# Early attention blocks: queries with places of their own, keys in pairs of blocks, and new durations in the plan of the first stage

## The chip, the core and the metric

The kernel runs on one core of a Trainium2 chip. The metric is the device time of one execution in microseconds (us); lower is better. A core has TensorE (matmuls, called PE in the profile, and its weight loads, PEld), VectorE (DVE), ScalarE (ACT), GpSimd (POOL) and SyncE (SP, which here issues most DMAs). Each engine takes its instructions in the order in which the program lists them and waits on semaphores for the others. TensorE accumulates in PSUM; everything else that is local lies in SBUF.

## The reference, cut to what matters

Three layers follow each other: attention with a window of 128 positions, a dense feed-forward layer, and a layer of 8 experts of which each token uses one.

```python
# q, k, v: (4, 8, 576, 64) float32
scores = scale * np.matmul(q, k.transpose(0, 1, 3, 2))
mask = (rel >= 0) & (rel < window)
scores = np.where(mask, scores + bias[None], -1000000000.0)
...
attn = attn / (np.sum(attn, axis=-1, keepdims=True) + 1e-09)
attn_out = np.matmul(attn, v)
# x: (2304, 512), w_in: (512, 2048), w_out: (2048, 512)
h = x @ w_in
g = h - np.tanh(h)
x = g @ w_out
# then: every token goes to the one of 8 experts with the largest logit
```

The 2304 tokens are 18 blocks of 128. A block's queries see the keys of their own block and of the block before (block 0, and others that start a sequence, see their own alone).

## The kernel before, in words

**The work.** The tokens go in groups of two blocks (a group is g, its blocks b = 2g and 2g + 1). For a block, `quarter` handles two heads at a time, so a block has four quarters (a = 4b + 0 to 3; the half hf names four heads, qq the pair in it, jj = 0, 1 the head of the pair). The heads of a pair lie in partitions 0 to 63 and 64 to 127 of the transposed queries and keys. A quarter makes scores on TensorE, adds the bias and takes the minimum of the negated scores on VectorE (`soft`, L479), takes the exponential on ScalarE (`exp`, L493), transposes the probabilities and multiplies them by the values. Then `x_out` (L628 to L641) transposes the block's output for the feed-forward layer, whose `step` handles one of eight pairs of feature blocks (fp): h = x w_in (L681), the nonlinearity on ScalarE and VectorE (L686 to L698), and the product with w_out into `acc` (L705).

**Early blocks.** Blocks 0 to 3 (NF = 4) are early: their attention is done in f32 (`early`), with transposes on TensorE (`tr_pe`, L513), copies out of PSUM (`tr_out`, L519) and f32 values (`pv_f`, L530). Their scores (L452) are one matmul of 128 columns for each head and key block; in the trace an f32 matmul leaves two records, a transpose one. Later blocks use another number format and a DMA transpose (`tr`, L508).

**Borrowed places.** Early data lies in the SBUF places of weights that are loaded later. A place is called by its tag: `wi12` holds w_in's feature block 12, `wo15` w_out's 15 (FT = 16 of each). Before the change, `wo15` and `wo14` hold the keys of blocks 0, 1 and 2, 3 (`kf[0]`, `kf[1]`, loaded by L391), `wi14` and `wi13` the values, and `wi15` a second buffer for probabilities. Queries (L395) have two places, `qst0` and `qst1`, each for half a block, used in turn, so a load must wait for the scores two halves before. The `slots` in `weight` name what must have been read before a weight may be loaded into its place.

**Weights.** The 32 weight blocks of the feed-forward layer come as 64-bit integers and are rebuilt by `weight`: a load (L298, L300), a conversion on ScalarE (L325), a scaling (L307 on ScalarE or L309 on VectorE), two joining instructions on VectorE (L328, L331), a rounded copy (L313) and a subtraction for the remainder (L317, on VectorE or GpSimd). Both halves must be there before `step` may use the block.

**The plan.** Nothing is issued while the tasks are described. `Plan.add` takes for each task the engines that may do it with a duration for each, a due time, and what it reads and writes. `Plan.order` then builds the whole program's order: again and again it takes, of all tasks whose inputs are ready, the one with the earliest start, then the earliest due time, then the first described, on the engine that would finish it first. A load on SP also waits until the modelled transfer pipe is nearly free. So the durations that tasks are given decide the order of the instructions on every engine, and where there is a choice the engine. `weights` and `qk_half` and `quarter` set due times from the step number p at which a block is wanted.

In `build`, group 0 gets four of the eight pairs first, then group 1 all eight, then group 0 the other four, then the other groups. The lines that decide a plan's choice are these:

```python
fin = {e: max(free.get(e, 0.0), r0) + c + ALPHA * load.get(e, 0.0) for e, c in eng.items()}
e = min(fin, key=fin.get)
st = max(free.get(e, 0.0), r0)
if e == "SP":
    st = max(st, pipe - AHEAD)
key = (st, due, n)
```

Of the kernel before, what the change touches and what calls it, by code (L numbers as in the profile page):

```python
# [10 lines left out]
F32 = mybir.dt.float32  # L11
# [22 lines left out]
FT = FF // 128  # L34
# [4 lines left out]
NF = 4  # L39
# [9 lines left out]
QK = 2  # L49
# [113 lines left out]
class Builder:  # L163
# [122 lines left out]
    def weight(self, P, j, kind, f, due):  # L286
# [31 lines left out]

        slots = [("kf", 2 * (FT - 1 - f) + x, y) for x in range(2) for y in range(2)] if kind == "o" else []
        if (kind, f) == ("i", FT - 1):  # L320
            slots = [("p32", 1, 0), ("p32", 1, 1)]
        elif kind == "i":
            slots = [("vf", 2 * (FT - 2 - f) + x) for x in range(2)]
        P.add({"SP": 1.46}, load, due - 2 - (EARLY if self.early() else 0), w=[raw, (raw, "L")] + slots)
        P.add({"ACT": 0.46}, lambda e: nc.scalar.activation(  # L325
            out=v["L"], in_=v["L"].bitcast(U32), func=AF.Copy, scale=7.499 * 2.0 ** -32), due, r=[raw], w=[(raw, "L")])
        P.add({"DVE": 0.335, "ACT": 0.46}, scale, due, r=[raw, "at"], w=[wf])
        P.add({"DVE": 0.6}, lambda e: nc.vector.scalar_tensor_tensor(  # L328
            out=v["L"], in0=v["H"], scalar=-2 ** 31, in1=v["L"], op0=ALU.bitwise_and, op1=ALU.bitwise_or),
            due, r=[raw], w=[(raw, "L")])  # L330
        P.add({"DVE": 0.6}, lambda e: nc.vector.scalar_tensor_tensor(  # L331
            out=fi, in0=fi, scalar=3, in1=v["L"], op0=ALU.logical_shift_left, op1=ALU.bitwise_or), due,
            r=[raw, (raw, "L"), "at"], w=[wf])
        P.add({"ACT": 0.46, "DVE": 0.335}, hi, due, r=[wf, "at"], w=[raw, (raw, "L"), (key, 0)])
        P.add({"DVE": 0.6, "POOL": 1.23}, lo, due, r=[wf, (key, 0), "at"], w=[(key, 1)])

# [8 lines left out]
    def qk_half(self, P, b, hf, due):  # L345
# [33 lines left out]
        if b >= NF:  # L379
            q, qn = ("q", b, hf), ("q", n)  # L380
            P.add({"SP": 0.73}, lambda e: load("q"), due - 2, r=["at"], w=[q, "stq"])
            P.add({"ACT": 0.52}, qcopy, due, r=["at", q, "stq"], w=[qn])
            P.add(sub, qsub, due, r=["at", qn, "stq"], w=[("ql", n)])
        else:
            s4 = b % 4

            def load_k0(e):
                if hf == 0 and s4 % 2 == 0 and b < 4:
                    self.kf[s4 // 2] = self.wp.tile([128, 2, 4, 128], F32, tag=f"wo{FT - 1 - s4 // 2}",
                                                    name=f"kf{s4 // 2}")  # L390
                nc.sync.dma_start(out=self.kf[s4 // 2][:, s4 % 2, hf * 2:hf * 2 + 2, :], in_=self.i["k0"][b, hf])  # L391

            def load_q0(e):
                self.qst[n] = self.at.tile([128, 2, 4, 128], F32, tag=f"qst{n}", name=f"qf{n}", bufs=1)
                nc.sync.dma_start(out=self.qst[n][:, 0, 0:2, :], in_=self.i["q0"][b, hf])  # L395

            P.add({"SP": 0.36}, load_k0, due - 2, r=["at"], w=[("kf", s4, hf)] + ([("kf", s4 + x, y) for x in range(2) for y in range(2)] if hf == 0 and s4 % 2 == 0 and b < 4 else []))
            P.add({"SP": 0.36}, load_q0, due - 2, r=["at"], w=[("q", n), ("ql", n)])

# [31 lines left out]
    def quarter(self, P, a, due):  # L431
# [13 lines left out]
        def scores(jj):  # L445
            sc = v["sc"][jj] = self.scores[jj][:, 0]
            q = self.qst[n]
            j = qq + 2 * jj
            hp, p0 = hf * 4 + j, 64 * jj
            if b < NF:  # L450
                for x in [b] if one else [b - 1, b]:
                    nc.tensor.matmul(sc[:, b - x, :], lhsT=q[p0:p0 + 64, 0, qq, :],  # L452
                                     rhs=self.kf[x % 4 // 2][p0:p0 + 64, x % 2, hf * 2 + qq, :], start=True, stop=True)
                return
            sl = s if one else slice(0, 2)
# [117 lines left out]
        q = [("q", n), ("ql", n)]  # L573
        ttr = 0.2 if one else (0.35 if s == 0 else 0.48)
        ttr += 0.13 * (2 * (b in SPLIT) + (b - 1 in SPLIT))
        for jj in range(2):
            if early:
                P.add({"PE": 0.4 if one else 0.8}, lambda e, jj=jj: scores(jj), due,
                      r=["at"] + [("kf", x % 4, hf) for x in ([b] if one else [b - 1, b])] + q, w=[("sc", jj)])
# [6 lines left out]
        for jj in range(2):  # L586
            P.add({"ACT": 0.33 if one else 0.45}, lambda e, jj=jj: exp(jj), due,
                  r=["at", ("sc", jj), ("mx", jj, a % 2)], w=[("p32", pb, jj), ("sm", sk, qq, jj)])
        sm = [("sm", sk, x, y) for x in range(2) for y in range(2)]
        half = [("xr", 2 * hf), ("xr", 2 * hf + 1)]  # L590
        if early:
            for jj in range(2):
                P.add({"PE": 0.15 if one else 0.25}, lambda e, jj=jj: tr_pe(jj), due, r=["at", "con", ("p32", pb, jj)],
                      w=[("tp", jj)])
            for jj in range(2):
                P.add({"ACT": 0.3, "DVE": 0.22} if one else {"ACT": 0.4, "DVE": 0.35}, lambda e, jj=jj: tr_out(e, jj),
                      due, r=["at", ("tp", jj)], w=[("pt", a % 2, 1)] if jj else [("pt", a % 2), ("pt", a % 2, 1)])
            P.add({"PE": 0.6 if one else 1.2}, pv_f, due,
                  r=["at", ("pt", a % 2), ("pt", a % 2, 1)] + [("vf", x) for x in ([b] if one else [b - 1, b])], w=[("o", qq)] if qq else ["o", ("o", 0), ("o", 1)])
            if qq:  # L600
                P.add({"DVE": 0.5}, recip, due, r=["at"], w=sm)
                P.add({"DVE": 0.4}, mul, due, r=["at", "o", ("o", 0), ("o", 1)] + sm, w=half if hf else [("xr", m) for m in range(4)])
            return
# [557 lines left out]
    def build(self):  # L1161
        tc, nc = self.tc, self.nc
        for n in ("kf", "vf", "sums", "oh4", "qst", "xr", "acc", "w"):
            setattr(self, n, {})
# [24 lines left out]
        for g, fps in visits:  # L1189
# [173 lines left out]
def layout(inputs):  # L1363
    f = np.float32

    def compact(x):
        y = np.asarray(x).reshape(B, 2, 4, S, D)[:, :, HPOS]
        y = y.transpose(1, 2, 4, 0, 3).reshape(2, 2, 2, D, NB, 128)[:, :, :, :, :NF]
        return np.ascontiguousarray(y.transpose(4, 0, 1, 3, 2, 5).reshape(NF, 2, 128, 256))

# [41 lines left out]
```

## Time and profile before

| what | value |
|---|---|
| median of 3 runs | 858.4 us (857.5 to 860.28) |
| the profiled execution | 856.46 us |
| its span, first to last instruction | 854.8 us |
| mean granted TensorE clock | 0.987 of 2.4 GHz |
| TensorE busy | 820.6 us (96%) |
| VectorE busy | 575.4 us (67%) |
| ScalarE busy | 437.9 us (51%) |
| GpSimd busy | 232.0 us (27%) |

The span lies 1.66 us below the execution's own time, which is counted from outside. Busy shares are averages over the whole span; the early attention, the rebuilding of the weights and the first feed-forward steps fill about the first 140 us, and what bounds the kernel there is read from that stretch alone. In the profile a matmul's end is modelled, so that the durations of neighbouring records overlap; the distance between their starts tells more. The granted clock is given in parts of 2.4 GHz: 1.00 is 2.4 GHz and 0.50 is 1.2 GHz. In the chain of waits each piece is what released the next; "issue" is time in which an engine waited for nothing that the profile shows.

### The profile page before, as it was taken

The page shows a single profiled execution, that of the slowest core. Times are in us where ns is not written, and L with a number is a line of the kernel's source. Part 1 is how long each engine was busy: PE and PEld are TensorE (multiplying, and loading weights), DVE is VectorE, ACT ScalarE, POOL GpSimd, SP SyncE. Part 2 cuts the span into 40 slices and gives each one's busy share as a digit, 9 for nine tenths or more (in the row PEclk, how much of TensorE's full clock was granted, in tenths as well). Part 3 has the DMA queues.
Part 4 walks back from the last instruction along what each step waited for, and adds up shares of the span by engine and source line. Part 5 has one row for each costly group of instructions (what it writes and reads, how often), then busy time and mean ns, then how long its engine had stood idle before and what let it go on. Part 6 is the DMA issues. An engine that isn't in the chain of part 4 may idle for free.

```text
span 854.8 us, 15357 instructions
## 1 busy us (share of the span) xinstructions
PE 820.6 (96%) x5292; PEld 731.2 (86%) x5292; DVE 575.4 (67%) x1525; ACT 437.9 (51%) x990; POOL 232.0 (27%) x228
## 2 busy tenths in 40 slices
PE   7998799999999999999999999999999999999995
PEld 5886688989889998898888898998889999989994
DVE  5688997777769567777677675577366655666230
ACT  4587765554555455555555543455255544545120
POOL 1255742133325123243333251022110110111011
PEclk9998799999999999999999999999999999999998
DMA  7786316934433234333334322265266655655000
GB/s 246 248 281 234 96 55 156 301 99 118 99 94 96 79 69 117 75 87 88 97 83 91 91 51 50 99 213 167 77 205 221 200 184 178 197 166 173 19 27 30
DMA packets 110327, 112.35 MB, mean 131 GB/s; under 512 B 62997, under 2 KB 77333, under 8 KB 110112
## 3 DMA queue, kind: packets, MB, share of 16 engines
q1 hardware_dynamic: 107104, 101.82, 41.8%
q0 software_dynamic: 3136, 9.46, 3.0%
q8 instruction: 43, 0.70, 0.3%
q14 instruction: 44, 0.36, 0.1%
HBM read 86.59 MB, written 17.48 MB: 122 GB/s over the span
## 4 chain that ended last, share of the span: by engine, by line
PE 73%; DVE 10%; issue 7%; DMA 6%; SPq 2%; ACT 2%; POOL 1%; POOLq 0%; ACTq 0%; DVEq 0%
PE h L681 19%; PE acc L705 17%; PE he L1009 10%; PE y L1044 8%; PE o L541 3%; DMA pt<-ph 3%; PE sc L452 3%; DVE wst L331 2%; DMA out<-yo,ix 2%; PE sc L457 2%; PE y L1040 2%; PE of L530 2%; PE misc L780 1%; SPq L914 1%; PE sc L513 1%
## 5 line engine op out<-in xcount | busy, mean ns | idle before, releaser
L681 PE MATMUL h<-xT,wi 128*128 128x256 f32 x1728 | 228.9, 287 | 0.0
L681 PEld LDWEIGHTS h<-xT,wi 128*128 128x128 f32 x1728 | 220.3, 194 | 5.2 <-issue 0.2
L705 PE MATMUL acc<-wo,gh 128*128 128x512 f32 x576 | 187.0, 406 | 0.6 <-ACT xspill L657 0.6
L705 PE MATMUL acc<-wo,gl 128*128 128x512 f32 x288 | 113.8, 395 | 0.1
L705 PEld LDWEIGHTS acc<-wo,gh 128*128 128x128 f32 x576 | 100.4, 191 | 15.1 <-ACT xspill L657 0.8
L686 ACT ACTIVATE t<-h 128x512 f32<-128x512 f32 x72 | 43.0, 597 | 113.6 <-PE h L681 113.5
L1044 PE MATMUL y<-eo,ge 128*128 128x512 f32 x336 | 88.5, 399 | 0.0
L479 DVE CUSTOM_DVE_ANT_0 sc<-sc,bias 128x256 f32<-128x256 f32 (+1 forms) x144 | 52.4, 375 | 44.4 <-PE sc L457 34.7
L493 ACT ACTIVATE p<-sc,mx 128x256 f32<-128x256 f32 (+1 forms) x128 | 59.1, 464 | 33.7 <-DVE mx L479 31.3
L1069 POOL DMA_INDIRECT out<-yo,ix x24 | 23.1, 964 | 177.2 <-PE y L1040 61.7
L698 DVE TENSOR_TENSOR gl<-t,gh 128x512 fp32r<-128x512 f32 x72 | 65.1, 904 | 7.4 <-ACT gh L694 7.3
L1044 PEld LDWEIGHTS y<-eo,ge 128*128 128x128 f32 x336 | 60.0, 188 | 9.7
L1031 DVE SCALAR_TENSOR_TENSOR ge<-he,ge 128x256 fp32r<-128x256 f32 x104 | 30.0, 326 | 54.7 <-ACT ge L1025 54.6
L705 PEld LDWEIGHTS acc<-wo,gl 128*128 128x128 f32 x288 | 54.6, 190 | 13.1 <-DVE gl L698 0.5
L943 DVE TENSOR_TENSOR eo<-est,eo 128x512 fp32r<-128x512 f32 x58 | 43.7, 755 | 27.0 <-ACT eo L939 25.1
L1025 ACT ACTIVATE ge<-he 128x320 fp32r<-128x320 f32 (+1 forms) x56 | 24.1, 430 | 71.5 <-PE he L1009 66.3
L1009 PE MATMUL he<-xT,ei 128*128 128x320 f32 x384 | 60.4, 309 | 0.0
L1009 PEld LDWEIGHTS he<-xT,ei 128*128 128x128 f32 x384 | 58.3, 188 | 2.3
L689 DVE TENSOR_TENSOR t<-h,t 128x512 f32<-128x512 f32 x72 | 49.4, 686 | 14.8 <-ACT t L686 14.5
L1009 PE MATMUL he<-xA,ei 128*128 128x320 f32 (+1 forms) x384 | 59.0, 302 | 0.0
L939 ACT CAST eo<-est 128x512 fp32r<-128x512 f32 x64 | 39.7, 621 | 36.8 <-PE y L1040 22.5
L1009 PEld LDWEIGHTS he<-xA,ei 128*128 128x128 f32 x384 | 56.3, 188 | 2.6
(182 smaller groups left out, 1409.6 us busy)
## 6 DMA issues: line engine op xcount, KB each, us to landing
est<-in_w SPq DMA_DIRECT2D x128, 256.0 KB
rawi<-in_w_in SPq DMA_DIRECT2D x16, 512.0 KB
rawo<-in_w_out SPq DMA_DIRECT2D x16, 512.0 KB
stk<-in_k SPq DMA_DIRECT2D x30, 256.0 KB
stq<-in_q SPq DMA_DIRECT2D x28, 256.0 KB
bucket<-in_c_pad SPq DMA_DIRECT2D x8, 771.0 KB
xe<-bucket SPq DMA_DIRECT2D x17, 257.0 KB
vst<-in_v SPq DMA_DIRECT2D x30, 128.0 KB
```

What stands on the lines that cost most here:

```text
L479: nc.vector.tensor_tensor_reduce(out=x, in0=x, in1=self.bias[:, h, c0:c1], scale=-0.125, scalar=mx[:, 1:2] if m else 3.0e38, op0=ALU.add, ...
L493: nc.scalar.activation(out=v["p32"][:, jj * W:(jj + 1) * W], in_=x, func=AF.Exp, scale=-1.0, bias=v["mx"][jj][:, 0:1], accum_out=self.sums ...
L681: nc.tensor.matmul(h3(v["h"], f2), lhsT=w[:, a, k, :], rhs=xT[c][:, :, k, :], start=(k == 0 and n == 0), stop=(k == KD - 1 and n == 2))
L686: nc.scalar.activation(out=v["t"], in_=v["h"].rearrange("p a b -> p (a b)"), func=AF.Tanh)
L689: nc.vector.tensor_tensor(out=v["t"], in0=v["h"].rearrange("p a b -> p (a b)"), in1=v["t"], op=ALU.subtract)
L698: self.eng(e).tensor_tensor(out=v["gl"], in0=v["t"], in1=v["gh"].bitcast(F32), op=ALU.subtract)
L705: nc.tensor.matmul(self.acc[g, t], lhsT=v[a][:, c0:c0 + 128], rhs=self.w["o", fs[f2]][:, c, :], start=(first and f2 == 0 and n == 0), stop ...
L939: nc.scalar.copy(out=t[:, 0, :], in_=v["x"])
L943: self.eng(eng).tensor_tensor(out=t[:, 1, :], in0=v["x"], in1=t[:, 0, :].bitcast(F32), op=ALU.subtract)
L1009: nc.tensor.matmul(h[:, 0:N], lhsT=w[:, a, c0:c0 + 128], rhs=xT()[b][:, k, 0:N], start=(k == 0 and n == 0), stop=(k == KD - 1 and n == 2))
L1031: nc.vector.scalar_tensor_tensor(out=g[:, o:o + c1 - c0], in0=hk[f][:, c0:c1], scalar=0.0, in1=g[:, c0:c1].bitcast(F32), op0=ALU.max, op1= ...
L1044: nc.tensor.matmul(y[t], lhsT=gt(f, a)[:, (t - ts[0]) * 128:(t - ts[0] + 1) * 128], rhs=self.w["o", f0 + f][:, b, :], start=(f == 0 and n ...
```

## The change

It has three parts. Queries of the early blocks get places for whole blocks: `wi12` for blocks 0 and 1, `wo12` for 2 and 3, one load for a block. Keys get a place for each pair of a block with the one before: `wo15` for blocks 0 and 1, `wo14` for 1 and 2, `wo13` for 2 and 3; blocks 2 and 3 load the block before once more. A head's scores then are one matmul of 256 columns (128 for block 0). Loads of the weights that follow into these places wait for their new readers (`slots`). The third part are the durations: those of the weights' tasks, of the softmax (for all blocks, the later ones too), and of the early blocks' matmuls and copies. The input arrays q0 and k0 are laid out for it on the host.

```diff
+        slots = {("i", FT - 1): [("p32", 1, 0), ("p32", 1, 1)], ("i", FT - 2): [("vf", 0), ("vf", 1)],
+                 ("i", FT - 3): [("vf", 2), ("vf", 3)], ("i", FT - 4): [("qf", 0), ("qf", 1)],
+                 ("o", FT - 4): [("qf", 2), ("qf", 3)]}.get(key, [])
+        if kind == "o" and 1 <= FT - f < NF:
+            slots = [("kf", FT - f, 0), ("kf", FT - f, 1)]
...
-        P.add({"ACT": 0.46}, lambda e: nc.scalar.activation(
+        P.add({"ACT": 0.68}, lambda e: nc.scalar.activation(
...
-        P.add({"DVE": 0.335, "ACT": 0.46}, scale, due, r=[raw, "at"], w=[wf])
-        P.add({"DVE": 0.6}, lambda e: nc.vector.scalar_tensor_tensor(
+        P.add({"DVE": 0.5, "ACT": 0.68}, scale, due, r=[raw, "at"], w=[wf])
+        P.add({"DVE": 1.0}, lambda e: nc.vector.scalar_tensor_tensor(
...
-        P.add({"DVE": 0.6}, lambda e: nc.vector.scalar_tensor_tensor(
+        P.add({"DVE": 0.92}, lambda e: nc.vector.scalar_tensor_tensor(
...
-        P.add({"ACT": 0.46, "DVE": 0.335}, hi, due, r=[wf, "at"], w=[raw, (raw, "L"), (key, 0)])
-        P.add({"DVE": 0.6, "POOL": 1.23}, lo, due, r=[wf, (key, 0), "at"], w=[(key, 1)])
+        P.add({"ACT": 0.62, "DVE": 0.47}, hi, due, r=[wf, "at"], w=[raw, (raw, "L"), (key, 0)])
+        P.add({"DVE": 0.95, "POOL": 1.45}, lo, due, r=[wf, (key, 0), "at"], w=[(key, 1)])
...
+    def qk_early(self, P, b, due):
+
+        nc, d2 = self.nc, b // 2
+
+        def load_k(e):
+            t = max(b, 1)
+            if b != 1:
+                self.kf[t] = self.wp.tile([128, 2, 4, 128], F32, tag=f"wo{FT - t}", name=f"kf{t}")
+            for x in ([b] if b < 2 else [b, b - 1]):
+                nc.sync.dma_start(out=self.kf[t][:, t - x], in_=self.i["k0"][x])
+
+        def load_q(e):
+            if b % 2 == 0:
+                self.qf[d2] = self.wp.tile([128, 2, 4, 128], F32, tag=f"w{'io'[d2]}{FT - 4}", name=f"qf{d2}")
+            nc.sync.dma_start(out=self.qf[d2][:, b % 2], in_=self.i["q0"][b])
+
+        P.add({"SP": 0.73}, load_q, due, r=["at"], w=[("qf", b)] + ([] if b % 2 else [("qf", b + 1)]))
+        P.add({"SP": 0.73 if b < 2 else 1.46}, load_k, due, r=["at"],
+              w=[("kf", 1, 0)] if b == 1 else [("kf", max(b, 1), 0), ("kf", max(b, 1), 1)])
...
-            if b < NF:
-                for x in [b] if one else [b - 1, b]:
-                    nc.tensor.matmul(sc[:, b - x, :], lhsT=q[p0:p0 + 64, 0, qq, :],
-                                     rhs=self.kf[x % 4 // 2][p0:p0 + 64, x % 2, hf * 2 + qq, :], start=True, stop=True)
+            if early:
+                x = slice(1, 2) if one else slice(0, 2)
+                nc.tensor.matmul(sc[:, 0:W // 128, :], lhsT=self.qf[b // 2][p0:p0 + 64, b % 2, hf * 2 + qq, :],
+                                 rhs=self.kf[max(b, 1)][p0:p0 + 64, x, hf * 2 + qq, :], start=True, stop=True)
                 return
...
-        ttr = 0.2 if one else (0.35 if s == 0 else 0.48)
+        ttr = 0.43 if one else (0.57 if cs == 0 else 0.8)
...
-                P.add({"PE": 0.4 if one else 0.8}, lambda e, jj=jj: scores(jj), due,
+                P.add({"PE": 0.45 if one else 0.65}, lambda e, jj=jj: scores(jj), due,
...
-            P.add({"ACT": 0.33 if one else 0.45}, lambda e, jj=jj: exp(jj), due,
+            P.add({"ACT": 0.57 if one else 0.67}, lambda e, jj=jj: exp(jj), due,
...
-                P.add({"PE": 0.15 if one else 0.25}, lambda e, jj=jj: tr_pe(jj), due, r=["at", "con", ("p32", pb, jj)],
+                P.add({"PE": 0.28 if one else 0.5}, lambda e, jj=jj: tr_pe(jj), due, r=["at", "con", ("p32", pb, jj)],
...
-                P.add({"ACT": 0.3, "DVE": 0.22} if one else {"ACT": 0.4, "DVE": 0.35}, lambda e, jj=jj: tr_out(e, jj),
+                P.add({"ACT": 0.3, "DVE": 0.29} if one else {"ACT": 0.38, "DVE": 0.42}, lambda e, jj=jj: tr_out(e, jj),
...
-            P.add({"PE": 0.6 if one else 1.2}, pv_f, due,
+            P.add({"PE": 0.85 if one else 1.65}, pv_f, due,
...
+                            self.qk_early(P, b, due - QK - 2)
```

## Rows read from the trace of the kernel before

**Rows 1.** The page's head and first part: busy us, share, instructions.

```profile
span 854.8 us, 15357 instructions
PE 820.6 (96%) x5292; PEld 731.2 (86%) x5292; DVE 575.4 (67%) x1525; ACT 437.9 (51%) x990; POOL 232.0 (27%) x228
```

**Rows 2.** Stretches: length, busy us (x) by engine, granted clock, DMA share, GB/s.

```profile
core 0: us, PE busy (x) PEld busy (x) DVE busy (x) ACT busy (x) POOL busy (x), PEclk, DMA share, GB/s
0.00:16.00 16.00, 9.66 (x35) 6.97 (x35) 8.57 (x39) 5.82 (x18) 2.07 (x26) 1.00 0.78 237
16.00:56.00 40.00, 40.00 (x163) 32.41 (x161) 29.23 (x73) 27.38 (x73) 15.04 (x13) 1.00 0.78 258
56.00:108.00 52.00, 41.83 (x246) 36.17 (x245) 49.72 (x81) 40.62 (x90) 31.76 (x22) 0.84 0.55 188
...
140.00:840.00 700.00, 694.53 (x4638) 625.59 (x4637) 460.04 (x1281) 343.75 (x769) 167.72 (x156) 1.00 0.43 122
```

**Rows 3.** The chain that ended last, early pieces: start us, us, what.

```profile
6.83 0.72 PE sc L452 x2
...
30.31 1.90 PE of L530 x8
32.21 0.43 PE sc L513 x2
32.63 1.15 PE sc L452 x4
33.78 0.62 PE sc L513 x2
...
125.43 0.69 DVE wo L317
```

**Rows 4.** TensorE's instructions in order of time: start us, us, what.

```profile
4.66 0.80 PE L452 MATMUL sc<-kf,qf 64*128 64x128 f32 x4 [4.66 <-DMA qf<-in_q]
...
6.76 0.79 PE L452 MATMUL sc<-kf,qf 64*128 64x128 f32 x2
...
17.71 0.53 PE L530 MATMUL of<-vf,ptf 128*128 128x64 f32 x2
...
52.08 2.79 PE L681 MATMUL h<-xT,wi 128*128 128x256 f32 x12
...
56.73 1.69 PE L681 MATMUL h<-xT,wi 128*128 128x256 f32 x12
...
71.49 2.91 PE L681 MATMUL h<-xT,wi 128*128 128x256 f32 x12
...
81.33 0.72 PE L452 MATMUL sc<-kf,qf 64*128 64x128 f32 x8
```

**Rows 5.** A stretch behind the first fall of the granted clock, columns as in rows 2.

```profile
68.00:74.00 6.00, 5.70 (x26) 5.48 (x26) 5.12 (x13) 4.33 (x11) 2.79 (x2) 0.52 1.05 391
```

**Rows 6.** Line 530's records, 16 to 52 us: duration ns, least, median, most.

```profile
L530 PE MATMUL of<-vf,ptf x48: 316/421/473, 17.7 to 48.4; 128*128 128x64 f32 x48
```

**Rows 7.** SyncE's queue, 0 to 140 us: us waited in total, times, longest.

```profile
SPq L395 <- PE sc L452: 20.4, 6, 7.5
```

**Rows 8.** TensorE's waits, 0 to 140 us: us in total, times, longest.

```profile
PE sc L513 <- ACT p32x L493: 4.9, 3, 3.7
PE sc L452 <- DMA qf<-in_q: 4.7, 1, 4.7
PE misc L628 <- DVE xr L567: 4.3, 2, 3.7
```

**Rows 9.** VectorE's instructions near 86 us: start us, us, what.

```profile
85.67 0.68 DVE L328 SCALAR_TENSOR_TENSOR rawo<-rawo 128x512 int32<-128x512 int32 x1
86.27 0.42 DVE L479 CUSTOM_DVE_ANT_0 sc<-sc,bias 128x256 f32<-128x256 f32 x1
...
89.64 1.79 DVE L328 SCALAR_TENSOR_TENSOR rawo<-rawo 128x512 int32<-128x512 int32 x1
```

**Rows 10.** TensorE's waits, 140 to 854 us, as in rows 8.

```profile
PE o L541 <- DMA pt<-ph: 4.1, 6, 1.0
```

More of the change, by code (lines that the diff above doesn't have):

```diff
@@ L317, in lo @@
             self.eng(e).tensor_tensor(out=t[:, 1, :], in0=f32, in1=t[:, 0, :].bitcast(F32), op=ALU.subtract)
[L319 to L323, printed above, removed]
+        slots = {("i", FT - 1): [("p32", 1, 0), ("p32", 1, 1)], ("i", FT - 2): [("vf", 0), ("vf", 1)],
[3 more added lines that the diff above has]
+            slots = [("kf", FT - f, 0), ("kf", FT - f, 1)]
         P.add({"SP": 1.46}, load, due - 2 - (EARLY if self.early() else 0), w=[raw, (raw, "L")] + slots)
-        P.add({"ACT": 0.46}, lambda e: nc.scalar.activation(
+        P.add({"ACT": 0.68}, lambda e: nc.scalar.activation(
             out=v["L"], in_=v["L"].bitcast(U32), func=AF.Copy, scale=7.499 * 2.0 ** -32), due, r=[raw], w=[(raw, "L")])
-        P.add({"DVE": 0.335, "ACT": 0.46}, scale, due, r=[raw, "at"], w=[wf])
-        P.add({"DVE": 0.6}, lambda e: nc.vector.scalar_tensor_tensor(
+        P.add({"DVE": 0.5, "ACT": 0.68}, scale, due, r=[raw, "at"], w=[wf])
+        P.add({"DVE": 1.0}, lambda e: nc.vector.scalar_tensor_tensor(
             out=v["L"], in0=v["H"], scalar=-2 ** 31, in1=v["L"], op0=ALU.bitwise_and, op1=ALU.bitwise_or),
             due, r=[raw], w=[(raw, "L")])
-        P.add({"DVE": 0.6}, lambda e: nc.vector.scalar_tensor_tensor(
+        P.add({"DVE": 0.92}, lambda e: nc.vector.scalar_tensor_tensor(
             out=fi, in0=fi, scalar=3, in1=v["L"], op0=ALU.logical_shift_left, op1=ALU.bitwise_or), due,
             r=[raw, (raw, "L"), "at"], w=[wf])
-        P.add({"ACT": 0.46, "DVE": 0.335}, hi, due, r=[wf, "at"], w=[raw, (raw, "L"), (key, 0)])
-        P.add({"DVE": 0.6, "POOL": 1.23}, lo, due, r=[wf, (key, 0), "at"], w=[(key, 1)])
+        P.add({"ACT": 0.62, "DVE": 0.47}, hi, due, r=[wf, "at"], w=[raw, (raw, "L"), (key, 0)])
+        P.add({"DVE": 0.95, "POOL": 1.45}, lo, due, r=[wf, (key, 0), "at"], w=[(key, 1)])
     def early(self):
@@ L383, in qk_half @@
             P.add(sub, qsub, due, r=["at", qn, "stq"], w=[("ql", n)])
[L384 to L398, printed above, removed]
+    def qk_early(self, P, b, due):
[13 more added lines that the diff above has]
+              w=[("kf", 1, 0)] if b == 1 else [("kf", max(b, 1), 0), ("kf", max(b, 1), 1)])
     def v_full(self, P, b, due):
@@ L446, in scores @@
             sc = v["sc"][jj] = self.scores[jj][:, 0]
-            q = self.qst[n]
             j = qq + 2 * jj
             hp, p0 = hf * 4 + j, 64 * jj
-            if b < NF:
-                for x in [b] if one else [b - 1, b]:
-                    nc.tensor.matmul(sc[:, b - x, :], lhsT=q[p0:p0 + 64, 0, qq, :],
-                                     rhs=self.kf[x % 4 // 2][p0:p0 + 64, x % 2, hf * 2 + qq, :], start=True, stop=True)
+            if early:
+                x = slice(1, 2) if one else slice(0, 2)
+                nc.tensor.matmul(sc[:, 0:W // 128, :], lhsT=self.qf[b // 2][p0:p0 + 64, b % 2, hf * 2 + qq, :],
+                                 rhs=self.kf[max(b, 1)][p0:p0 + 64, x, hf * 2 + qq, :], start=True, stop=True)
                 return
+            q = self.qst[n]
             sl = s if one else slice(0, 2)
@@ L577, in quarter @@
             if early:
-                P.add({"PE": 0.4 if one else 0.8}, lambda e, jj=jj: scores(jj), due,
-                      r=["at"] + [("kf", x % 4, hf) for x in ([b] if one else [b - 1, b])] + q, w=[("sc", jj)])
+                P.add({"PE": 0.45 if one else 0.65}, lambda e, jj=jj: scores(jj), due,
+                      r=["at", ("qf", b)] + [("kf", max(b, 1), x) for x in ([1] if one else [0, 1])], w=[("sc", jj)])
             else:
@@ L1162, in build @@
         tc, nc = self.tc, self.nc
-        for n in ("kf", "vf", "sums", "oh4", "qst", "xr", "acc", "w"):
+        for n in ("kf", "qf", "vf", "sums", "oh4", "qst", "xr", "acc", "w"):
             setattr(self, n, {})
@@ L1368, in compact @@
         y = y.transpose(1, 2, 4, 0, 3).reshape(2, 2, 2, D, NB, 128)[:, :, :, :, :NF]
-        return np.ascontiguousarray(y.transpose(4, 0, 1, 3, 2, 5).reshape(NF, 2, 128, 256))
+        return np.ascontiguousarray(y.transpose(4, 1, 3, 0, 2, 5).reshape(NF, 128, 4, 128))
     def tr(x):
```

## The prediction

> **What bounds the kernel now.** I went from the page to stretches, then to the chain of waits, then to single instructions. The page: TensorE is busy 820.6 of 854.8 us [rows 1], so the end can move only where TensorE idles, runs slowly or gets less to do. The table of stretches shows where that is [rows 2]. From 140 to 840 us TensorE is busy 694.5 of 700 us. From 16 to 56 us it is busy all 40.00 us, with VectorE at 29.23. From 56 to 108 us VectorE is busy 49.72 of 52 and TensorE 41.83. So there are two early bounds: TensorE during the softmax attention of blocks 0 to 2, then VectorE, which joins the weights' two integer halves. Whatever ends earlier there, the full queue of matmuls behind it ends earlier by.
>
> From 30.31 us the chain is TensorE alone [rows 3]: a quarter of two heads costs 1.90 (probabilities times values) + 0.43 + 1.15 + 0.62 + 1.15 (transposes and scores in turn, the second head's scores as the first's) = 5.25 us.
>
> The clock has to be read with care. The granted clock stands at 1.00 (2.4 GHz) in the rows up to 56 us [rows 2], yet twelve records of h take 2.79 us at 52.08 and 1.69 at 56.73 [rows 4]; at 71.49 they take 2.91 in a stretch whose granted clock is 0.52, mostly the 1.2 GHz level [rows 4, 5]. By the durations all of 16 to 54 us ran at the lower level; it rose after the first run of full-width h matmuls. It fell again behind idle time: 0.52 from 68 to 74 us [rows 5], and the whole of 56 to 108 us has 0.84 [rows 2].
>
> **The change, part by part.** *Keys in pairs.* For a block that sees two key blocks, each head's scores are now one matmul of 256 columns instead of two of 128. A matmul in f32 leaves two records, so four records of 128 become two of 256. What is a record of 256 worth? At the low level a head with four records holds the chain for 1.15 us and one with two for 0.72 [rows 3], so one more record of 128 columns costs 0.215. Two readings are open. If weights are the limit, 256 columns also cost 0.215, as the 256-column records of h do: (2.79 - 0.42) / 11 = 0.215, with 0.42 for the last one [rows 4, 6]. If columns are the limit, they cost 0.43 and nothing is saved. The row that decides is the pair of 64-column records at 17.71, 0.53 us in all [rows 4]: the second begins 0.53 - 0.42 = 0.11 after the first, because its weights had been loaded early. So 64 columns of f32 take 0.11, two clocks a column at 1.2 GHz, and 128 take 0.215 with nothing left over. I take 0.43 for 256: the merge itself is worth **0**. The other end is 0.43 less a head.
>
> By the Trainium skill ("TensorE: Matmul & The Clock Gate", Back-to-back issue gap) consecutive matmuls are N/1.2 ns apart on the cold clock, one clock a column; that gives 0.21 us for 256 columns and would make the merge worth 0.43 a head. The pair at 17.71 speaks against it for f32; no run so far shows 256 columns of f32.
>
> *The two heads of a quarter side by side.* They lie in partitions 0 to 63 and 64 to 127. Where both heads' scores follow each other they overlap: four records of two heads take 0.80 us at 4.66 and two records of one head 0.79 at 6.76 [rows 4]: the second head is free. So in a quarter whose heads are split by a transpose, 1.15 us is lost at the low level. From 16 to 52 us all fourteen heads stand alone as at 32.63, a transpose before and behind [rows 3]: seven quarters, up to 7 x 1.15 = 8.05 us. Does the new plan put them together? The plan places by earliest start, then due time. It had charged 1.2 for the probabilities times values; now 1.65, and an exponential 0.67 instead of 0.45. While the 1.65 run, both heads' exponentials can end; then the two transposes and the two scores are all ready when TensorE comes free, and equal due times leave the scores adjacent. With the old charges the second head was not ready in time, so a transpose came between. Weight instructions on VectorE can still part them; I take four quarters of seven, **-4.6**; ends 0 and -8.05. VectorE has 10.8 us free in that stretch and the DMA share is 0.78 [rows 2], so both can follow into 35 us; without that room the term is nothing.
>
> *Queries in places of their own.* Eight loads of 128 KB become four of 256 KB, and none waits for an earlier reader. SyncE's queue stood 20.4 us in six such waits, the longest 7.5 [rows 7], with weight loads queued behind. TensorE did not wait on these except for the first load, and VectorE, not the data, is late after 56 us. I take 0; an earlier weight could save up to the two stalls below.
>
> *What it adds on queues.* Two further key loads of 256 KB (blocks 2 and 3 fetch the block before again): 0.5 MB at 258 GB/s [rows 2] is 2 us of transfer, taken as 0 beside the freed SyncE time; otherwise 2 us that delay weights. The first scores now need 512 KB instead of 256 KB. TensorE waited 4.7 us for the smaller loads [rows 8]; 0.25 MB more at the 237 and 258 GB/s of the first stretches [rows 2] costs 1.0 to 1.1, less if the transfers are not yet at their pace: **+0.9**, in full, nothing covers it. All eight query and key transfers have early due times, so the first weight starts behind them by about 1.5 MB more, 5 us; VectorE is idle then (8.57 of 16 us busy [rows 2]).
>
> *Weights in the borrowed places.* Two more weights of the last two of eight pairs wait for block 3's scores (the last begin at 81.33 us [rows 4]). They are needed by the second token group's last steps, after 140 us; hidden, unless SyncE holds other loads behind them.
>
> *The plan's times.* The joining instructions were planned at 0.6 and are now 0.92 to 1.0; they took 0.68 alone and 1.79 beside a GpSimd subtraction [rows 9]. Because the plan ran ahead of VectorE, weight work stood ahead of a softmax at 86.27, and TensorE waited 3.7 us for its probabilities; 3.7 more for the block's output near 100 us [rows 8]. True charges should let the softmax, with its earlier due time, go first. That is 7.4 us if both go. But VectorE's work stays the same, so part returns as later weights: I take a third, **-2.5**; ends +4 (one more stall of that size) and -7.4. The longer softmax charges also hold for the later blocks, where TensorE waits 4.1 us in six waits on transposed probabilities [rows 10]; a reordering there can cost or win about that. I take 0.
>
> **Sum.** The profiled execution took 856.46 us (span 854.8). -4.6 + 0.9 - 2.5 = -6.2 gives 850.3; its time lies 1.9 below the median of 858.4, so a median of about **852**. A difference under 0.3% (2.6 us) can't be told from none.
>
> **Rivals.** *A. Columns at one clock* (0.08). The merge saves 0.43 a head; with heads overlapping, 9 quarters at the low level x 0.43 and 3 x 0.21 (half, on twice the clock) = 4.5 us more: 847.5. For it: h's records. Against: the pair of 64 columns. This is the time that the page of the Trainium skill named above would give.
>
> *B. VectorE absorbs it* (0.18). The scores pair up, but the end of the weights' work, near 126 us [rows 3], stays, since VectorE was busy nearly throughout from 56 us and its instructions are the same; TensorE only idles more. Then only the first load and small shifts remain: 858, no change. Against it: VectorE's 10.8 idle us before 56.
>
> *C. Slower through the clock* (0.16). As B, and TensorE, with less to do beside a full VectorE, idles longer between 50 and 108 us and falls to the lower level more often. A stretch like 68 to 74 us costs half its length [rows 5], about 3 us; two more and the first load's 0.9 make 858.4 + 6.9 = 865. It decides once idle time ahead of h grows past the 10 us that TensorE has there now. For it: the clock fell behind stalls of under 4 us.
>
> *D. The heads stay apart* (0.14): no pairing and no better order, the merge worth 0: +0.9 to -2.5, about 858.
>
> **Chances.** Forecast 0.44, A 0.08, B 0.18, C 0.16, D 0.14. The forecast and A are faster; so is part of D and B, where single terms remain, for 0.60 in all; no change 0.22; slower 0.18. The range: down to 844 (858.4 - 8.05 - 7.4 + 0.9), up to 862, which takes in B, D and the smaller half of C; about 1 in 10 lies outside on either side.
>
> **What would show it.** Right: score records fall from 112 to 64; a 256-column record starts about 0.43 us after its partner at the low level; both heads adjacent in most quarters, a quarter near 4.1 us instead of 5.25; no wait of SyncE on a query load; block 2 ends 4 to 5 us sooner; no stall of 3.7 us before the transposes; TensorE saturated from about 130 instead of 136 us. Wrong: records of 256 columns 0.21 apart (A); VectorE's last joining instruction still near 126 us (B); granted clock low for much more than 17 us (C); transposes still between the heads (D).

## The result and the profile after

The changed kernel takes 848.02 us (median of 4 runs, 845.91 to 849.56). The kernel before, run beside it on the same chip, takes 858.31 (4 runs). The ratio is 0.9885 with a 95% interval of 0.986 to 0.9909. It is 10.3 us faster where 6.2 were forecast. The profiled execution took 849.56 us, the slowest of the four.

The head of the page, as in [rows 1]: TensorE is busy 3.9 us less and the span is 7.0 us shorter.

```profile
span 847.8 us, 15246 instructions
PE 816.7 (96%) x5244; PEld 721.2 (85%) x5244; DVE 565.5 (67%) x1500; ACT 441.6 (52%) x997; POOL 252.1 (30%) x246
```

The stretches of the changed kernel, with the columns of [rows 2]:

```profile
0.00:16.00 16.00, 9.51 (x34) 6.82 (x34) 7.10 (x34) 5.36 (x18) 3.33 (x27) 1.00 0.87 287
16.00:56.00 40.00, 39.00 (x132) 26.78 (x130) 24.48 (x68) 25.47 (x70) 11.58 (x11) 1.00 0.95 332
56.00:108.00 52.00, 48.78 (x292) 40.50 (x292) 46.05 (x78) 42.96 (x96) 26.27 (x17) 1.00 0.37 127
108.00:140.00 32.00, 29.95 (x196) 26.70 (x194) 31.34 (x41) 23.38 (x45) 25.09 (x18) 1.00 0.27 79
...
140.00:200.00 60.00, 57.33 (x430) 51.63 (x428) 49.10 (x153) 37.92 (x96) 32.22 (x33) 1.00 0.73 194
200.00:300.00 100.00, 99.19 (x714) 88.92 (x713) 71.43 (x208) 50.66 (x129) 37.20 (x35) 1.00 0.38 92
```

Read against [rows 2], the gain lies in one stretch. From 16 to 56 us TensorE is nearly as full as before (39.00 against 40.00 us), with fewer records. From 56 to 108 us it idles 3.2 us instead of 10.2, and the granted clock is 1.00 instead of 0.84. VectorE is busy 4.75 us less from 16 to 56 us and 3.7 less from 56 to 108: part of its weight work has moved back, and part has gone to ScalarE and GpSimd (of the weights' 96 scalings, rounded copies and remainders, which two engines can do, VectorE has 10, before 18).

Where TensorE's work stands shows the same from its own side. The matmul h that starts at 152.69 us here is the one that started at 161.32 before, counted by full groups of h: 8.6 us ahead. The values of block 1, however, end at nearly the same time (their last record starts at 42.1 us against 42.3), and those of block 2 later (69.8 against 63.6).

TensorE's waits from 0 to 140 us, as in [rows 8]:

```profile
PE sc L456 <- DMA kf<-in_k: 5.5, 1, 5.5
...
PE misc L633 <- DVE xr L572: 1.7, 1, 1.7
...
PE sc L518 <- ACT p32x L498: 0.4, 1, 0.4
```

Both stalls of 3.7 us are gone: the wait on the probabilities (p32x) falls from 4.9 to 0.4 us, the one on the block's output (xr) from 4.3 to 1.7. The first scores wait 5.5 us for data instead of 4.7.

### The profile page after: what moved, and what is told of

It reads as the page before. It is cut to its first block, busy times and chain, and to the rows that moved or that the text cites. A ratio compares the mean times of both kernels' runs of the same rounds, so it can differ in the third digit from the quotient of the medians.

```text
span 847.8 us, 15246 instructions
## 1 busy us (share of the span) xinstructions
PE 816.7 (96%) x5244; PEld 721.2 (85%) x5244; DVE 565.5 (67%) x1500; ACT 441.6 (52%) x997; POOL 252.1 (30%) x246
## 4 chain that ended last, share of the span: by engine, by line
PE 71%; DVE 11%; DMA 7%; issue 6%; ACT 2%; SPq 2%; POOL 1%; POOLq 0%; DVEq 0%; ACTq 0%
PE h L686 19%; PE acc L710 17%; PE he L1014 9%; PE y L1049 8%; PE o L546 3%; DMA pt<-ph 3%; PE sc L456 3%; PE sc L462 2%; DMA out<-yo,ix 2%; DVE wst L331 2%; PE y L1045 2%; PE misc L785 2%; PE of L535 2%; DVE rawo L328 1%; PE sc L518 1%
## 5 line engine op out<-in xcount | busy, mean ns | idle before, releaser
L710 PE MATMUL acc<-wo,gh 128*128 128x512 f32 x576 | 183.9, 400 | 0.0
L508 POOL TENSOR_TENSOR ph<-p,ph 128x512 f16<-128x512 f32 (+1 forms) x38 | 46.1, 1214 | 69.3 <-ACT ph L503 26.0
L703 DVE TENSOR_TENSOR gl<-t,gh 128x512 fp32r<-128x512 f32 x72 | 63.0, 876 | 4.6 <-ACT gh L699 4.4
```

The source lines that it names most:

```text
L508: self.eng(e).tensor_tensor(out=ph[:, 2 * W:4 * W], in0=v["p32"][:, 0:2 * W], in1=ph[:, 0:2 * W], op=ALU.subtract)
L703: self.eng(e).tensor_tensor(out=v["gl"], in0=v["t"], in1=v["gh"].bitcast(F32), op=ALU.subtract)
L710: nc.tensor.matmul(self.acc[g, t], lhsT=v[a][:, c0:c0 + 128], rhs=self.w["o", fs[f2]][:, c, :], start=(first and f2 == 0 and n == 0), stop ...
```

## The experiments

Twelve kernels, measured in three groups of four, each beside the kernel before. That kernel took 857.39, 857.23 and 857.52 us in these groups, 0.8 to 1.1 below the result's own, so differences under 1 us aren't read. "To after" is the difference to the median of 848.02.

| kernel | what it is | us | ratio to before [95%] | to after |
|---|---|---|---|---|
| e1_times_only | before, with all the new durations | 843.31 | 0.9833 [0.981, 0.9856] | -4.7 |
| e2_places_only | after, with all the old durations | 862.03 | 1.0051 [1.0034, 1.0067] | +14.0 |
| e3_split_scores | after, keys unmerged | 848.38 | 0.9882 [0.9856, 0.9908] | +0.4 |
| e4_heads_together | after, two heads' scores as one task | 844.26 | 0.9837 [0.9814, 0.9861] | -3.8 |
| e5_weight_times | after, only the weights' durations new | 853.26 | 0.994 [0.9922, 0.9959] | +5.2 |
| e6_pe_times_old | after, early matmuls' durations old | 850.83 | 0.9939 [0.9917, 0.9962] | +2.8 |
| e7_weights_old | after, weights' durations old | 860.04 | 1.0034 [1.0021, 1.0046] | +12.0 |
| e8_times_heads | e1 with the edit of e4 | 847.77 | 0.9874 [0.9852, 0.9897] | -0.3 |
| e9_loads_later | after, loads of blocks 1 to 3 later | 848.0 | 0.9886 [0.9869, 0.9902] | 0.0 |
| e10_late_old | after, later blocks' softmax durations old | 856.83 | 0.9984 [0.9965, 1.0004] | +8.8 |
| e11_two_numbers | before, two joins' durations new | 854.3 | 0.9969 [0.9943, 0.9995] | +6.3 |
| e12_half_loads | after, first loads in halves | 846.4 | 0.9857 [0.9841, 0.9874] | -1.6 |

**The two halves of the change apart.** e1 takes the durations alone; e2 keeps the places and takes the durations back. These lines show the form; the rest are the other lines of the diff's third part.

```diff
# e1, on the kernel before
-        P.add({"DVE": 0.6}, lambda e: nc.vector.scalar_tensor_tensor(
+        P.add({"DVE": 1.0}, lambda e: nc.vector.scalar_tensor_tensor(
...
-            P.add({"PE": 0.6 if one else 1.2}, pv_f, due,
+            P.add({"PE": 0.85 if one else 1.65}, pv_f, due,
# e2, on the kernel after: the same lines turned back
```

> The kernel before with all the new durations of the plan, and the old places, loads and score matmuls. Theory P (the new order of the instructions made the gain): 847 to 851 us, no TensorE wait of over 2.5 us between 56 and 108 us, granted clock 1.00 in 72 to 108 us. Theory Q (the places made it, because weight loads no longer stand behind waiting query loads on SyncE): 856 to 860 us, with the 3.7 us waits and the falls of the clock still there.

> The kernel after with all the old durations: only places, loads and the 256-column scores are new. Theory P: 856 to 861 us (the first scores 0.8 us later, nothing gained). Theory Q: 847 to 851 us.

The durations alone win 14.1 us and the places alone lose 4.6, both clear of 1 by their intervals. The sum, -9.5, is the change within 0.8 us. So the gain is all from the numbers in the plan; e1 beats both kernels and is the best version run. Stretches of e1:

```profile
16.00:56.00 40.00, 39.91 (x165) 32.87 (x166) 27.52 (x69) 27.08 (x74) 14.10 (x12) 1.00 0.92 321
56.00:108.00 52.00, 47.29 (x334) 41.02 (x335) 50.73 (x82) 45.50 (x99) 29.49 (x21) 1.00 0.40 139
140.00:200.00 60.00, 60.00 (x455) 54.51 (x454) 49.84 (x152) 35.03 (x88) 29.21 (x29) 1.00 0.73 188
```

VectorE is nearly as full from 56 to 108 us as before (50.73 against 49.72), yet TensorE does 334 records there instead of 246, at a granted clock of 1.00 instead of 0.84: a VectorE as full as before no longer holds TensorE up. SyncE's waits of e1 from 0 to 140 us:

```profile
SPq L395 <- PE sc L452: 21.8, 6, 7.0
```

The fastest kernel keeps the waits on the query loads [rows 7] that the places removed.

e2 has the places without the durations. Its stretch from 56 to 108 us:

```profile
56.00:108.00 52.00, 38.63 (x213) 31.46 (x214) 51.90 (x83) 39.45 (x88) 28.45 (x21) 0.87 0.54 184
```

And TensorE's waits in it, 0 to 140 us:

```profile
PE sc L518 <- ACT p32x L498: 5.8, 4, 2.0
PE misc L633 <- DVE xr L572: 5.8, 2, 5.2
```

The two kinds of stall of [rows 8] stand here again, longer in all than before (5.8 us each, against 4.9 and 4.3).

**The merge alone.** e3 writes the 256-column matmul as two of 128 and leaves the rest.

```diff
-                nc.tensor.matmul(sc[:, 0:W // 128, :], lhsT=..., rhs=self.kf[max(b, 1)][p0:p0 + 64, x, ...], ...)
+                for y in [0] if one else [1, 0]:
+                    x = 1 if one else y
+                    nc.tensor.matmul(sc[:, y, :], lhsT=..., rhs=self.kf[max(b, 1)][p0:p0 + 64, x, ...], ...)
```

> The kernel after, with each 256-column score matmul written as two of 128 again; order, places and durations stay. If the merge is worth nothing because f32 columns take two clocks each: within 1 us of the kernel after (847 to 850), and four records of 128 columns take the same 1.22 us as the two of 256. If the merge is worth 0.43 us a head at the lower clock: 5 to 9 us slower, 853 to 857.

848.38 against 848.02: nothing. TensorE's instructions in the changed kernel, in order of time, show why:

```profile
5.46 0.80 PE L456 MATMUL sc<-kf,qf 64*128 64x128 f32 x4 [5.46 <-DMA kf<-in_k]
...
28.82 1.23 PE L456 MATMUL sc<-kf,qf 64*128 64x256 f32 x4
30.63 1.97 PE L535 MATMUL of<-vf,ptf 128*128 128x64 f32 x8 [0.58 <-DVE ptf L524]
32.39 0.64 PE L518 MATMUL sc<-con,p 128*128 128x128 f32 x2
32.95 1.22 PE L456 MATMUL sc<-kf,qf 64*128 64x256 f32 x2
34.10 0.69 PE L518 MATMUL sc<-con,p 128*128 128x128 f32 x2
34.72 1.22 PE L456 MATMUL sc<-kf,qf 64*128 64x256 f32 x2
35.87 1.97 PE L535 MATMUL of<-vf,ptf 128*128 128x64 f32 x8
37.63 1.06 PE L518 MATMUL sc<-con,p32x 128*128 128x128 f32 x4
38.78 1.80 PE L456 MATMUL sc<-kf,qf 64*128 64x256 f32 x4
...
50.08 2.93 PE L686 MATMUL h<-xT,wi 128*128 128x256 f32 x12
...
62.31 2.93 PE L686 MATMUL h<-xT,wi 128*128 128x256 f32 x12
65.03 1.47 PE L535 MATMUL of<-vf,ptf 128*128 128x64 f32 x8
...
67.51 1.71 PE L686 MATMUL h<-xT,wi 128*128 128x256 f32 x12
```

(The last four lines are read further below.) Two records of 256 columns take 1.22 us where two of 128 took 0.79 [rows 4]: 0.215 more for each 128 columns added. And e3, in the same place, from its own instructions:

```profile
32.34 1.22 PE L457 MATMUL sc<-kf,qf 64*128 64x128 f32 x4
33.49 0.69 PE L519 MATMUL sc<-con,p 128*128 128x128 f32 x2
34.11 1.22 PE L457 MATMUL sc<-kf,qf 64*128 64x128 f32 x4
```

Four records of 128 columns take the same 1.22. The Trainium skill ("TensorE: Matmul & The Clock Gate", Back-to-back issue gap) has N/1.2 ns between matmuls on the cold clock, its word for the lower level; these f32 rows show twice that.

**The heads side by side, by force.** e4 makes both heads' scores one task of the plan; e8 does it on e1.

```diff
-                P.add({"PE": 0.45 if one else 0.65}, lambda e, jj=jj: scores(jj), due, ..., w=[("sc", jj)])
+                if jj == 0:
+                    P.add({"PE": 0.8 if one else 1.25}, lambda e: (scores(0), scores(1)), due, ...,
+                          w=[("sc", 0), ("sc", 1)])
```

> The kernel after, with both heads' scores of an early quarter as one task of the plan, so that they always stand side by side. If TensorE bounds the stretch up to 60 us: about ten quarters x 1.15 us less, 838 to 843 us, block 1 ends near 36 instead of 40.5 us. If VectorE and the waits between engines absorb it: 846 to 850 us, TensorE idle between 16 and 56 us grows by what the scores save.

> The kernel before with all the new durations (as in the first run) and both heads' scores of an early quarter as one task of the plan; old places, four records of 128 columns a head. If the side by side heads are worth what they were on the kernel after (3.8 us) and add to the durations: 838 to 841 us. If VectorE and the waits between engines absorb them: 842 to 845.

On the changed kernel it wins 3.8 us, on e1 it loses 4.5 (e8 against e1). The pairs save time on TensorE, but that time doesn't reach the end by itself. The stretch from 16 to 56 us of e4:

```profile
16.00:56.00 40.00, 33.51 (x138) 24.08 (x139) 33.54 (x75) 30.95 (x80) 16.57 (x13) 1.00 1.02 362
```

And its TensorE waits, 0 to 140 us:

```profile
PE sc L518 <- ACT p L498: 3.9, 5, 1.8
PE sc L518 <- ACT p32x L498: 3.0, 4, 1.6
PE of L535 <- ACT ptf L524: 2.9, 6, 0.7
```

TensorE now idles 6.5 us in a stretch where the changed kernel idled 1.0, and waits for the softmax and the copies out of the transposes. By these waits the next work of a quarter is ready only when VectorE and ScalarE have done theirs, so their part of the chain sets the pace there. e8 is alike (33.40 us busy); its granted clock from 56 to 108 us is 0.93 where e1's is 1.00, which can cost up to 0.07 x 52 = 3.6 us of its loss (an estimate).

Nor do e4's 3.8 us show what the pairs are worth. The last values record of its block 1 starts at 44.16 us, 2.1 later than in the changed kernel, and its first h at 49.68 against 50.08. Its lead arises behind that, where its h runs at the upper level already, while in the changed kernel h still takes 2.93 us at 62.31:

```profile
54.58 1.69 PE L688 MATMUL h<-xT,wi 128*128 128x256 f32 x12
```

**Which durations.** On the changed kernel, e5 turns back all but the weights' numbers, e6 the early scores, transposes and values, e7 the weights' numbers, e10 the softmax numbers of the later blocks alone. e11 puts two numbers into the kernel before.

```diff
# e6
-            P.add({"PE": 0.85 if one else 1.65}, pv_f, due,
+            P.add({"PE": 0.6 if one else 1.2}, pv_f, due,
# e7 (and five lines like it)
-        P.add({"DVE": 1.0}, lambda e: nc.vector.scalar_tensor_tensor(
+        P.add({"DVE": 0.6}, lambda e: nc.vector.scalar_tensor_tensor(
# e10
-        ttr = 0.43 if one else (0.57 if cs == 0 else 0.8)
+        ttr = (0.43 if one else 0.57) if early else (0.2 if one else (0.35 if s == 0 else 0.48))
-            P.add({"ACT": 0.57 if one else 0.67}, ...
+            P.add({"ACT": (0.57 if one else 0.67) if early else (0.33 if one else 0.45)}, ...
# e11, on the kernel before: the joins 0.6 -> 1.0 (L328) and 0.6 -> 0.92 (L331), nothing else
```

> The kernel after, with only the weights' durations new; softmax, transposes, scores and values keep their old ones. If the weights' durations alone make the new order (VectorE's joins no longer stand ahead of a softmax): 847 to 851 us, no wait of over 3 us between 56 and 108 us. If the matmuls' durations make it: 856 to 862 us.

> The kernel after, with the old durations for the early blocks' matmuls and transposes only (scores 0.8, transposes 0.25, values 1.2). If the weights' durations alone make the gain: 847 to 851 us. If the matmuls' durations make it: 856 to 862 us. Both needed: 851 to 856.

> The kernel after, with the old durations for the weights' tasks only. If the weights' durations make the gain: 856 to 862 us, with TensorE waits of 3 us or more and falls of the granted clock between 56 and 108 us. If the matmuls' durations make it: 847 to 851 us.

> The kernel after, with the old softmax durations for the later blocks 4 to 17 and the new ones for the early blocks. If the new durations cost something behind 140 us (TensorE waits there 8.0 us after, 5.1 before): 845 to 847 us. If they help there too or do nothing: 848 to 851.

> The kernel before with two durations changed and nothing else: the joining instructions on VectorE at 1.0 and 0.92 instead of 0.6. If the plan's lag behind VectorE is what made the stalls and the falls of the clock: 846 to 852 us, no TensorE wait of over 3 us and granted clock 0.95 or more between 56 and 108 us. If it takes the whole set of durations: 855 to 859 us.

Without the weights' numbers the change is a loss (e7, 860.0). With them alone it is 8.8 us better than with none (e2 to e5). The early matmuls' numbers are worth 2.8 by the medians (e6; its ten runs spread from 848.1 to 856.1, so the size is loose). The two joins' numbers alone, on the kernel before, give 3.2 us with an interval that nearly touches 1. The single losses, 12.0 + 8.8 + 2.8 = 23.6, are more than the 14.0 of all together: each set of numbers gives a new order, and the orders don't add.

e7 from 56 to 108 us:

```profile
56.00:108.00 52.00, 38.61 (x203) 31.68 (x202) 51.90 (x84) 37.63 (x87) 33.58 (x24) 0.79 0.42 140
```

Its TensorE waits, 56 to 140 us:

```profile
PE of L535 <- DVE ptf L524: 4.5, 1, 4.5
PE sc L518 <- ACT p32x L498: 4.0, 4, 2.4
```

With weights charged too little, VectorE is full (51.90 of 52 us) and the attention's copies and softmax stand behind weight work. TensorE idles 13.4 us instead of 3.2 and the granted clock is 0.79.

The durations also choose engines, and no run holds that choice fixed while the order changes. Of the 96 instructions of the weights that two engines can do, VectorE has 18 before, 10 in the changed kernel, 12 in e1, 24 in e7 and 2 in e11. Its weight instructions take 74.0 us before, 68.0 in the changed kernel, 74.3 in e1, 80.9 in e7 and 65.4 in e11. So e7 also has more to do on VectorE. But less load on VectorE isn't enough for the gain: e1 has as much as before and gains 14.1 us, e11 has the least of all and gains 3.2.

e10 loses elsewhere. At 153 us it stands where the changed kernel stands (the h at 152.69 starts at 153.0). Its stretches behind that, which compare with the last two of the changed kernel's table:

```profile
140.00:200.00 60.00, 54.96 (x394) 48.65 (x395) 48.56 (x157) 32.64 (x86) 23.60 (x24) 0.97 0.74 185
200.00:300.00 100.00, 96.16 (x688) 86.91 (x687) 70.26 (x205) 49.72 (x126) 32.66 (x31) 0.98 0.39 92
```

And its TensorE waits from 140 us on:

```profile
PE o L546 <- DMA pt<-ph: 8.0, 9, 2.1
PE sc L462 <- ACT p L498: 3.7, 3, 2.2
```

The same two rows of the changed kernel:

```profile
PE o L546 <- DMA pt<-ph: 4.6, 6, 1.7
PE sc L462 <- ACT p L498: 2.0, 2, 1.4
```

The old numbers add 5.1 us of waits on transposed probabilities and on exponentials, and the clock is no longer full (0.97 and 0.98). These are block 4 and later, which the new places and the merged keys don't touch. In the kernel before, which had the old numbers everywhere, the same stretches are full:

```profile
140.00:200.00 60.00, 59.53 (x436) 53.73 (x435) 45.39 (x144) 33.16 (x82) 16.18 (x16) 1.00 0.67 189
200.00:300.00 100.00, 99.83 (x725) 90.20 (x724) 74.49 (x213) 51.61 (x133) 33.18 (x33) 1.00 0.37 91
```

So the new numbers of the later blocks don't gain anything on the kernel before there (TensorE idles 0.6 us before, 3.5 in the changed kernel); by these rows it is the mixture of new and old that loses.

**What the places cost.** e9 moves the loads of blocks 1 to 3 three steps back, so that the first weight isn't behind them. e12 loads block 0's queries and keys in halves, so that the first scores can start.

```diff
# e9
-                            self.qk_early(P, b, due - QK - 2)
+                            self.qk_early(P, b, due - QK - 2 + (3 if b else 0))
# e12
+        if b == 0:
+            P.add({"SP": 0.36}, lambda e: half("q", 0), due, ...)
+            P.add({"SP": 0.36}, lambda e: half("k", 0), due, ...)
+            P.add({"SP": 0.36}, lambda e: half("q", 1), due + 0.5, ...)
+            P.add({"SP": 0.36}, lambda e: half("k", 1), due + 0.5, ...)
+            return
```

> The kernel after, with the query and key loads of blocks 1 to 3 due 3 steps later in the plan, so that the first weights and values may go ahead of them. If the new places cost their 4.7 us because 2.5 MB of queries and keys go ahead of the first weight (its conversion starts at 16.5 instead of 13.5 us): 844 to 846 us, with that conversion near 13.5 us. If not: 847 to 850.

> The kernel after, with block 0's queries and keys loaded in halves of four heads (128 KB each, as before), the first halves first. The first scores start near 4.7 instead of 5.46 us. If that delay passes to the end in full, as the prediction took it: 846.8 to 847.6 us, 0.8 less than the kernel after. If it is lost in the waits behind it: 847.5 to 849.

e9 has its first weight conversion at 11.9 us (16.5 in the changed kernel, 13.5 before) and gains nothing. e12 starts its scores at 4.85 us instead of 5.46 and gains 1.6, which its interval (0.9841 to 0.9874, against 0.986 to 0.9909) does not quite separate from nothing. So the late first weight is not what the places cost; the late first scores may be a third of it. Even that third isn't isolated: in e12 h takes 1.69 us at 56.00 already, and the granted clock is 0.93 from 56 to 108 us and 0.97 from 140 to 200.

## Why the prediction was right, and where its sum was not

The direction and the range held; the sum was 4 us short, because two of its terms were off in opposite directions.

**Keys in pairs: 0 forecast, 0 measured** (e3). The reading of the 64-column pair, two clocks a column in f32, was right, and rival A falls: a record of 256 columns takes 0.43 us, twice one of 128. (In the trace its partner starts 0.59 us after it, and of two 128-column records of one head 0.375; the same 0.16 stands on top in both.) The 256-column records of h, 0.215 apart, are another case: the kernel keeps their operands as float32r, those of the early scores as plain float32, and the profile prints f32 for both. Score records fell to 64, as forecast, at no gain, in the table of groups by form, 0 to 140 us:

```profile
L456 PE MATMUL sc<-kf,qf 64*128 64x256 f32 x48 | 21.2, 617 | 0.1
L456 PE MATMUL sc<-kf,qf 64*128 64x128 f32 x16 | 5.6, 497 | 5.5 <-DMA kf<-in_k 5.5
```

**Two heads of a quarter side by side: -4.6 forecast, about -1.3 by the rows of two quarters.** This step failed. The mechanism is there (four records of 256 columns at 28.82 take 1.23 us, as long as two), but the plan put the heads together in two of seven quarters. At 28.82 the next work then waited 0.58 us for a copy, at 38.78 the four records took 1.80: 2.44 - 1.23 - 0.58 and 2.44 - 1.80 make 1.3 us. In the other five the heads stand apart, as at 32.95 and 34.72, and from 30.63 to 35.87 that is 5.24 us, the old 5.25. Block 1's values ended 0.2 us sooner, after a start 0.80 later; those of block 2, which the prediction had 4 to 5 us sooner, ended 6.2 later. That charging 1.65 for the values would leave both heads ready at once was argued from the plan's rule and did not come about; e1 keeps the same pattern, with one such pair. e4 and e8 show what the full pairing does: the time goes into waits for the softmax and the copies, so the end of -8.05 was not had there either, and the prediction's premise, that VectorE with 10.8 us free can follow into 35 us, did not hold.

**Queries in places of their own: 0 forecast.** SyncE's waits are gone, and they were worth nothing, as e1 has 21.8 us of them and is the fastest. In their place, as the prediction had left open, weights for the borrowed places now hold the queue, by SyncE's waits of the changed kernel, 0 to 140 us:

```profile
SPq L300 <- PE sc L456: 20.1, 2, 10.6
```

**First scores later: +0.9 forecast, +0.80 in the trace** (5.46 against 4.66), and 1.6 at the end by e12. But the places and loads together, which the sum had at +0.9, cost 4.6 (e2 to before) or 4.7 (after to e1). This term was mis-sized. Of the rest, e9 excludes the late first weight (3.0 us later, where the prediction had 5). What stands beside it between the changed kernel and e1 is the clock. The changed kernel stayed at the lower level some ten microseconds longer: in its instructions shown above h takes 2.93 us up to 62.31 us and 1.71 only at 67.51, and the eight records of the values in between, at 65.03, took 1.47, between the 1.97 of the lower level and the 1.00 of the upper. In e1 the change lies between these lines:

```profile
53.68 1.80 PE L530 MATMUL of<-vf,ptf 128*128 128x64 f32 x8
...
56.52 3.13 PE L681 MATMUL h<-xT,wi 128*128 128x256 f32 x24
59.49 1.00 PE L530 MATMUL of<-vf,ptf 128*128 128x64 f32 x8
```

Ten microseconds at 1.2 GHz instead of 2.4 are worth up to 5, about the 4.7 that separate the two. But e3 comes near to moving the rise alone, and speaks against so simple a sum: TensorE takes its tiles in the order of the changed kernel, and its clock rose 4 to 5 us sooner, before this line:

```profile
61.56 1.70 PE L687 MATMUL h<-xT,wi 128*128 128x256 f32 x12
```

The h that starts at 152.69 us in the changed kernel starts at 151.0 there, 1.7 ahead, and at 148.5 in e1; yet the span of e3 ends at 848.5, 0.7 later. So the late rise may explain part of the 4.7, and how much of it reaches the end isn't shown. It can't be the cause between e2 and the kernel before, where h takes 1.69 us at 55.84 and at 56.73 [rows 4]. There TensorE idles 13.4 us instead of 10.2 from 56 to 108 us, in the longer stalls shown above. Why the places lengthen them stays open.

**The plan's times: -2.5 forecast, -14 measured** (e1: -14.1; e2 to after: -14.0). This term was mis-sized by most. The prediction named the mechanism, weight work ahead of a softmax, and the two stalls that would go; they went. Its reason for taking a third, that VectorE's work stays the same and returns as later weights, was wrong. The weights did come later, by the last joining instruction of the changed kernel:

```profile
137.58 1.45 DVE L331 SCALAR_TENSOR_TENSOR wst<-wst,rawo 128x512 int32<-128x512 int32 x1
```

(at 124.1 us before, 129.4 in e1), and it cost nothing that the gain didn't cover. That also refutes rival B: the end of the weights' work was not the bound. That it was their place in VectorE's order is what the stalls in e2 and e7 speak for, and the shorter ones in e1 (1.3 us on p32x, 1.5 on xr, from 0 to 140 us); the choice of engines is not held apart from it. TensorE had other h to do while late weights were joined. Two further parts were not in the 7.4 us that the prediction took as the most. One is the clock, which fell in the same stretch, rival C with the other sign: a granted clock of 0.84 takes up to 0.16 x 52 = 8.3 us of full-clock time, 6.7 at TensorE's busy share of 0.80 in [rows 2], and it is 1.00 now (0.79 again in e7). The other is the later blocks' softmax numbers, taken at 0 with an end of 4: turned back alone they cost 8.8 (e10), so the rest's gain needs them, though they add none of their own behind 140 us. A reading of the prediction was also wrong: the 0.68 us at 85.67 [rows 9] was not alone, as a GpSimd subtraction ran beside it from 85.87 us on; the joining instruction at 85.07, with GpSimd idle, took the same 0.68.

The stretch adds up nearly, in an estimate: 7.0 us less idle and 6.7 for the clock, less 5 for the late rise, give 8.7; the h at 152.69 us is 8.6 ahead. That it agrees so closely is luck, as 1.0 us more idle from 16 to 56 us and the 1.3 of the pairs are left out. Behind that, TensorE idles 3.5 us from 140 to 300 us where it idled 0.6 before, and the span ends 7.0 ahead. The medians stand further apart than the spans, 10.3, since the profiled run of before was below its median (856.46) and that of after above (849.56).

Rival D had the heads right and the plan's times wrong. TensorE was not saturated from 130 us, as the list of signs had it: it idles 2.05 us from 108 to 140 and 2.67 from 140 to 200 us, where e1 is busy 60.00 of 60.00.

So it was luck that the total came out near the forecast, by two errors that partly cancelled: -4.6 and +0.9 became the +4.6 of e2 (+4.7 from e1 to the changed kernel), and -2.5 became the -14.1 of e1.

## What to carry to other kernels

Where a list scheduler orders the work, wrong durations can cost more than new code saves: take them from the trace, as means beside the engines that contend, and for every block that shares them, then test the numbers alone before new code goes with them. A merged matmul saves nothing where columns are the limit, as in f32 here, and a wait taken out of a queue (20 us here) is worth nothing if nobody needs what stands behind it sooner. An instruction saved on the bounding engine counts only as far as the engine that feeds it can follow; make that sum for both engines in the stretch, not by free time alone.

## What the runs showed of the hardware that was not expected

TensorE's clock rose for the first time at different points of nearly the same work. h took 2.93 us up to 62.31 us in the changed kernel; in e3, with the same order but unmerged scores, it took 2.93 at 57.26 and 1.70 at 61.56; in e1 24 of its records took 3.13 from 56.52 us. TensorE was busy 39.00, 39.01 and 39.91 of the 40 us from 16 to 56. Whether the order, the records or the single execution sets the point is not shown, as one execution of each kernel is profiled. The granted clock's column says 1.00 in all three, so a first rise is read from durations alone. The mean granted clock differs between runs of one kernel, too: six of e6's ten took 848.1 to 850.9 us at 0.995 to 0.996, four took 853.8 to 856.1 at 0.986 to 0.992.
